# Loading `a` into a block-structured tile, so that one DVE multiply makes AN with its zeros

## The chip, the cores and the metric

The kernel runs on one core of a Trainium2 chip. The metric is the device time of one execution, in microseconds (us). Its engines are PE (matmul), DVE (vector), ACT (scalar), POOL (GpSimd) and SP, which here only issues DMAs; each works through its own instruction order and waits for the others by semaphores.

## The reference

A recurrent attention over 4 batches, 8 heads, 768 steps and a head width of 40, and behind it two feed-forward layers over the 3072 tokens:

```
for t in range(768):
    y[t]  = r[t] @ state
    Sa    = state @ a[t]
    state = state * w[t] - outer(Sa, b[t]) + outer(v[t], k[t])
x = y as (3072, 320)
h = x @ w_in;  x = (max(h,0) + alpha*min(h,0)) @ w_out        # width 2048
out = (silu(x @ w_gate) * (x @ w_val)) @ moe2_w_out           # width 1536
```

All data is float32.

## The kernel before

The 768 steps are cut into 6 blocks of 128 steps; a block and a batch make an item, 24 in all (`order`, m the block, bb the batch). An item's eight heads lie in four pairs: one head of a pair in partitions 0 to 39 (`lo`), the other in 64 to 103 (`hi`), and its 128 steps are two chunks of 64. The step by step recurrence is replaced, within a chunk, by small matrices.

`load` (line 445) brings an item's inputs from HBM: `raw_wa` holds w and a of both halves, `raw_bk` holds b and k. `load_next` is called behind the code that last reads a tile, so the load for a later item waits for that reader. `rset` gives two sets of these tiles for the first eight items and one set afterwards. `prep_a` (492) builds the running products of w: ACT copies w into `wseg` (497), DVE scans it into `rest` (502) and `Wx` (509). Then it makes `AN`, a tile of two halves by 128 partitions: POOL clears the two quarters where half and partitions do not belong together (517), and two DVE multiplies on 64 partitions each write a times Wx into the other two (519). `prep_b` (525) multiplies b and k (`kbt`, 531), forms AN^T-like products on PE (`mnp`, 543), copies masked pieces of them into the cleared quarters of AN (ACT 556, POOL 557), and transposes kbt (571) into `KB` (574). `inverse` (586) inverts a block's triangular matrices in a chain of 31 short DVE steps (604, 612) between transposes (589, 615, 617) and two PE steps (`eps` 625, `dps` 644). `seq` (661) is the recurrence itself over the chunks of an item, as a chain through PE, ACT, DVE and POOL: `sp` 707, `zp` 714, `pp` 724 and 730, `gp` 741, `yp` 756 and 760. Two items run side by side, so there are two such chains.

Beside this, `conv` (187) rewrites the weights into two-part float32r (`narrow`, DVE 172 to 177), and `mlp1` (301) does the first feed-forward layer of a block once its attention is finished: `u` (238) and `d` (243 to 249) matmuls, in 16 groups of eight u and eight d for a block. Where one block's groups end and the next block's begin, the new block's x is fetched from HBM (`fill_x`, 257); below this place is called a seam. The second feed-forward layer (955 to 976) comes last.

The order on each engine is not written out by hand. The code gives every piece a priority (`tc.cur_priority`, `drive`, line 120), and the scheduler that builds the program picks for each engine among what is ready. A small edit can therefore change the order everywhere behind it.

Of the kernel before, what the change touches and what calls it, by code (L numbers as in the profile page):

```python
# [7 lines left out]
F32 = mybir.dt.float32  # L8
# [3 lines left out]
ALU = mybir.AluOpType  # L12
# [22 lines left out]
ANP = 0  # L35
# [27 lines left out]
L = 64  # L63
# [5 lines left out]
def kernel(  # L69
# [15 lines left out]
    nc = tc.nc  # L85
    NM, B, _, D, NP, TB = r.shape
# [3 lines left out]
    CPB = TB // L  # L90
    NSEG = NP * CPB
# [6 lines left out]
    lo, hi = slice(0, 64), slice(64, 128)  # L98
# [275 lines left out]
    def masks():  # L374
        nc.gpsimd.memset(mask, 1.0)
        for p in (lo, hi):
            nc.gpsimd.affine_select(
                out=mask[p], in_=mask[p], compare_op=ALU.is_gt, fill=0.0, base=0,
                pattern=[[1, L]], channel_multiplier=-1,
            )  # L380
        nc.gpsimd.memset(ident, 1.0)
        nc.gpsimd.affine_select(
            out=ident, in_=ident, compare_op=ALU.is_equal, fill=0.0, base=0,
            pattern=[[-1, 128]], channel_multiplier=1,
        )
# [7 lines left out]
    item_x = boot.enter_context(tc.tile_pool(name="item_x", bufs=XI, side="right"))  # L393
    raw = {}
    for j, pool in ((0, rawp), (1, bp)):
        for nm in ("wa", "bk"):
            t = raw[nm, j] = pool.tile([128, 2, NP, TB], F32, name=f"raw_{nm}{j}")
            for n in range(2):
                for q in (1, 3):
                    eng = nc.vector if nm == "wa" and j == 0 else nc.gpsimd  # L400
                    eng.memset(t[32 * q:32 * q + 32, n], 1.0 if (nm, n) == ("wa", 0) else 0.0)
        if j == 0:
            masks()
        tc.cur_priority += 10000
# [3 lines left out]
    for j in range(2):  # L408
        if j < NVT or BVT:
            t = (pers if j < NVT else bp).tile([128, NP, TB], F32, name=f"raw_vt{j}")  # L410
# [16 lines left out]
    for j in range(2):  # L427
        t = pers.tile([128, NG, L], F32, name=f"tt{j}")
        TT.append(t)
    ST = []  # L430
    for j in range(B):
        t = pers.tile([128, NP, 64], F32, name=f"ST{j}")
# [5 lines left out]
    seg = "q p (c t) -> q (p c) t"  # L438
# [3 lines left out]
    def rset(i):  # L442
        return i % 2 if i < EARLY else 0

    def load(i, nm):
        if i >= len(order):
            return
        m, bb = order[i]
        t = raw[nm, rset(i)]
        for h, pr in enumerate(halves):  # L450
            nc.sync.dma_start(out=t[pr], in_={"wa": wa, "bk": bk}[nm][m, bb, h])

    def load_next(i, nm):
        if i < EARLY - 2:
            load(i + 2, nm)
        elif i != EARLY - 1:
            load(i + (2 if i == EARLY - 2 else 1), nm)
# [34 lines left out]
    def prep_a(i):  # L492
        m, bb = order[i]
        it = items[i] = {}
        rw = raw["wa", rset(i)][:, 0]
        w3 = wseg[:, 0:WN].rearrange("p (s t) -> p s t", t=L + 1)
        nc.scalar.copy(out=w3[:, :, 1:L + 1], in_=rw.rearrange(seg, c=CPB)[:, :, ::-1])
        rest = rests[i % 2]
        fl = "p s t -> p (s t)"
        HW = WN // 2  # L500
        for g in range(2):
            nc.vector.tensor_tensor_scan(
                rest.rearrange(fl)[:, g * HW:g * HW + HW], wseg[:, g * HW:g * HW + HW], reset.rearrange(fl),
                0.0, ALU.mult, ALU.add,
            )
        item_p = item_x if i < XI else item_q
        wx = it["Wx"] = item_p.tile([128, NSEG, L + 1], F32, tag="Wx", name="Wx")
        nc.vector.reciprocal(out=first[:, ::-1, 0:1], in_=rest[:, :, L:L + 1])
        nc.vector.tensor_tensor_scan(
            wx.rearrange(fl), wseg[:, WN:0:-1], first.rearrange(fl), 0.0, ALU.mult, ALU.add  # L510
        )
        nc.scalar.copy(out=wx[:, ::-1, L:L + 1], in_=rest[:, :, L:L + 1])
        yield
        ra = raw["wa", rset(i)][:, 1]
        an = it["AN"] = item_p.tile([128, 2, NSEG, L], F32, tag="AN", name="AN")
        for h, pr in ((0, hi), (1, lo)):
            nc.gpsimd.memset(an[pr, h], 0.0)  # L517
        for h, pr in ((0, lo), (1, hi)):
            (nc.gpsimd if i >= B and ANP >> h & 1 else nc.vector).tensor_tensor(
                out=an[pr, h], in0=ra[pr].rearrange(seg, c=CPB), in1=wx[pr, ::-1, 0:L], op=ALU.mult  # L520
            )
        load_next(i, "wa")
        yield

# [256 lines left out]
    def preps(idx):  # L781
        yield from prep_a(idx[0])
        for i in idx:
            ga = prep_a(i + 1) if i + 1 in idx else iter(())
            for _ in prep_b(i):
                next(ga, 0)
                yield

    for i in range(2):
        load(i, "wa")  # L790
        load(i, "bk")
# [79 lines left out]
    for m in range(1, NM):  # L871
# [8 lines left out]
        nm = N_MLP + (1 if FA and m == 1 else 0)  # L880
# [150 lines left out]
```

## Time and profile before

| | |
|---|---|
| three runs, median (lowest to highest) | 1245.16 us (1241.27 to 1247.08) |
| profiled execution, first to last instruction (its span) | 1243.4 us |
| PE busy | 1095.8 us, 88% |
| DVE busy | 781.3 us, 63% |
| ACT busy | 592.6 us, 48% |
| POOL busy | 312.6 us, 25% |
| DMA, mean over the span | 134 GB/s |

The time of the profiled execution beyond its span is not listed; the span lies 1.8 us under the median and between the lowest and the highest run. The page is read by stretches: in the first 80 us there is hardly work for PE, up to about 248 us DVE is nearly full, and from there PE is.

### The profile page before, as it was taken

How to read it: one execution, taken by the hardware profiler on the slowest of the kernel's cores; microseconds unless marked ns; L12 is line 12 of the kernel's file. 1: busy time of each engine (PE TensorE's matmuls, PEld its weight loads, DVE VectorE, ACT ScalarE, POOL GpSimd, SP SyncE). 2: the span in 40 equal slices, each digit the busy share in tenths (PEclk: the TensorE clock that was granted, in tenths of full speed). 3: DMA queues.
4: the chain of work that ended last, by engine and by line, in shares of the span. 5: the costliest groups of instructions: out<-in, count | busy, mean ns of one | idle time of the engine just before them, and what ended most of it. 6: DMA issues, size and time to landing. Idle time of an engine off the chain costs nothing.

```text
span 1243.4 us, 24467 instructions
## 1 busy us (share of the span) xinstructions
PE 1095.8 (88%) x9056; PEld 928.7 (75%) x9056; DVE 781.3 (63%) x1689; ACT 592.6 (48%) x1463; POOL 312.6 (25%) x502
## 2 busy tenths in 40 slices
PE   3345787899799989989999899999999999999998
PEld 2244577777687777777777687888888888888887
DVE  7999999898669758974967444677732323232222
ACT  4547448844763674477455533455432323232222
POOL 9425443613121222252126300334500000000000
PEclk9658697999899999999999999999999999999999
DMA  5534577874545454464448648865210101000000
GB/s 149 168 115 133 180 257 251 263 228 126 161 127 176 134 161 142 144 196 145 145 139 266 201 131 292 283 213 153 73 47 1 47 1 38 1 22 1 22 1 22
DMA packets 92486, 166.36 MB, mean 134 GB/s; under 512 B 12752, under 2 KB 42704, under 8 KB 92368
## 3 DMA queue, kind: packets, MB, share of 16 engines
q1 hardware_dynamic: 84208, 160.87, 41.2%
q10 hardware_dynamic: 8160, 3.93, 1.1%
q8 instruction: 72, 1.18, 0.4%
q14 instruction: 46, 0.38, 0.1%
HBM read 136.98 MB, written 27.79 MB: 133 GB/s over the span
## 4 chain that ended last, share of the span: by engine, by line
PE 52%; DVE 20%; ACT 10%; DMA 8%; issue 6%; POOL 3%; SPq 1%; ACTq 0%; DVEq 0%; POOLq 0%
PE pg L238 10%; PE pv L238 10%; PE u L238 8%; PE o L952 3%; PE o L951 3%; PE o L953 3%; DVE la L612 3%; DVE tmp L604 3%; DMA raw_wa<-in_wa_dram 2%; PE gp L741 2%; PE d L243 2%; DMA xa<-xd 2%; PE d L244 2%; PE d L245 2%; DVE gs L685 2%
## 5 line engine op out<-in xcount | busy, mean ns | idle before, releaser
L184 ACT CAST gh<-g 128x512 fp32r<-128x512 f32 (+1 forms) x176 | 105.9, 602 | 175.2 <-DVE g L967 116.7
L967 DVE TENSOR_TENSOR g<-pv,sg 128x512 f32<-128x512 f32 x72 | 49.8, 691 | 200.1 <-PE pv L238 200.0
L185 DVE TENSOR_TENSOR gl<-g,gh 128x512 fp32r<-128x512 f32 (+1 forms) x176 | 119.5, 679 | 77.0 <-ACT gh L184 76.2
L238 PE MATMUL u<-xh,wt 128*128 128x512 f32 (+1 forms) x416 | 147.6, 397 | 15.9 <-DVE g L278 12.6
L278 DVE SCALAR_TENSOR_TENSOR g<-g,neg,u 128x512 f32<-128x512 f32 (+1 forms) x104 | 72.9, 701 | 63.0 <-ACT g L277 62.4
L238 PEld LDWEIGHTS u<-xh,wt 128*128 128x128 f32 x416 | 79.0, 193 | 34.9 <-DVE g L278 16.8
L238 PE MATMUL pg<-xh,w 128*128 128x512 f32 x288 | 102.0, 394 | 0.7 <-ACT sg L965 0.7
L965 ACT ACTIVATE sg<-pg 128x512 f32<-128x512 f32 x72 | 43.0, 597 | 124.3 <-PE pg L238 124.3
L238 PE MATMUL pv<-xh,w 128*128 128x512 f32 x288 | 100.5, 389 | 0.0
L277 ACT ACTIVATE g<-u 128x512 f32<-128x512 f32 (+1 forms) x104 | 58.7, 564 | 81.6 <-PE u L238 65.0
L543 PE MATMUL mnp<-AN,kbt 128*128 128x128 f32 x384 | 60.7, 311 | 32.1 <-POOL la L591 15.9
L952 PE MATMUL o<-w,gh 128*128 128x320 f32 x288 | 87.7, 309 | 0.0
L951 PE MATMUL o<-w,gh 128*128 128x320 f32 x288 | 87.1, 308 | 0.0
L244 PE MATMUL d<-gl,wt 128*128 128x512 f32 (+1 forms) x208 | 80.9, 391 | 1.2 <-DVE gl L185 1.2
L699 POOL COPY gs<-raw_v 64x160 f32<-64x160 f32 x96 | 42.3, 441 | 157.7 <-PE yp L756 70.1
L543 PEld LDWEIGHTS mnp<-AN,kbt 128*128 128x128 f32 x384 | 54.3, 219 | 36.2 <-POOL AN L517 17.6
L604 DVE TENSOR_TENSOR tmp<-la 128x96 f32<-128x96 f32 (+43 forms) x306 | 78.6, 281 | 3.2 <-POOL la L592 1.3
L238 PE MATMUL u<-xl,wt 128*128 128x512 f32 (+1 forms) x208 | 80.2, 386 | 0.2 <-DVE xl L185 0.2
L612 DVE TENSOR_TENSOR la<-la,tmp 128x96 f32<-128x96 f32 (+43 forms) x306 | 77.6, 278 | 1.9
L245 PE MATMUL d<-gh,wt 128*128 128x512 f32 (+1 forms) x208 | 78.5, 380 | 0.0
L557 POOL TENSOR_SCALAR_AFFINE_SELECT AN<-AN 64x256 f32<-64x256 f32 x96 | 48.5, 505 | 117.9 <-ACT AN L556 88.8
L953 PE MATMUL o<-w,gl 128*128 128x320 f32 x288 | 76.1, 309 | 0.0
(118 smaller groups left out, 2678.6 us busy)
## 6 DMA issues: line engine op xcount, KB each, us to landing
wt<-wd SPq DMA_DIRECT2D x98, 384.0 KB
wt<-wd SPq DMA_DIRECT2D x98, 320.0 KB
wd<-wc SPq DMA_DIRECT2D x24, 384.0 KB
raw<-in_moe_w_out_dram SPq DMA_DIRECT2D x28, 320.0 KB
raw_wa<-in_wa_dram SPq DMA_DIRECT2D x48, 160.0 KB
raw_bk<-in_bk_dram SPq DMA_DIRECT2D x48, 160.0 KB
wd<-wc SPq DMA_DIRECT2D x20, 320.0 KB
raw<-in_moe_w_in_dram SPq DMA_DIRECT2D x16, 256.0 KB
```

The lines of the kernel that those rows point to most:

```text
L184: nc.scalar.copy(out=h, in_=raw)
L185: eng.tensor_tensor(out=l, in0=raw, in1=h.bitcast(F32), op=ALU.subtract)
L238: nc.tensor.matmul(ps, lt, rh, start=(i == 0), stop=(i == len(ops) - 1))
L244: nc.tensor.matmul(ps, wh, gl, start=False, stop=False)
L245: nc.tensor.matmul(ps, wl, gh, start=False, stop=last)
L278: nc.vector.scalar_tensor_tensor(g, g, neg[:, f:f + 1], ps, ALU.mult, ALU.add)
L543: nc.tensor.matmul(ps[:, s].rearrange("p h t -> p (h t)"), kbt[:, g * SH + s].rearrange("p j t -> p (j t)"), an[:, :, g * SH + s, :],)
L604: nc.vector.tensor_tensor(out=tv, in0=ml[:, kk + 1:HALF, kk:kk + 1].to_broadcast([128, nr, ns]), in1=tl[:, kk:kk + 1, c0:c0 + ns].to_broad ...
L612: mark["inv"] = nc.vector.tensor_tensor(out=dst, in0=dst, in1=tv, op=ALU.subtract)
L951: nc.tensor.matmul(ops[q], gh[:, ts], wh, start=first, stop=False)
L952: nc.tensor.matmul(ops[q], gh[:, ts], wl, start=False, stop=False)
L953: nc.tensor.matmul(ops[q], gl[:, ts], wh, start=False, stop=last)
```

## The change

`raw_wa` becomes two tiles. `raw_w` holds w. `raw_a` has two halves over all 128 partitions, is cleared once, and each load writes only a head's own half: zeros stay where half and partitions do not belong together. One DVE multiply over 128 partitions and both halves then writes the whole of AN, its zeros too; the two POOL clears and the two 64-partition multiplies of each item go. Each load of w and a becomes two loads of half the size.

```diff
-        for nm in ("wa", "bk"):
-            t = raw[nm, j] = pool.tile([128, 2, NP, TB], F32, name=f"raw_{nm}{j}")
-            for n in range(2):
+        for nm in ("w", "bk"):
+            sh = [128, 2, NP, TB] if nm == "bk" else [128, 1, NP, TB]
+            t = raw[nm, j] = pool.tile(sh, F32, name=f"raw_{nm}{j}")
+            for n in range(sh[1]):
                 for q in (1, 3):
-                    eng = nc.vector if nm == "wa" and j == 0 else nc.gpsimd
-                    eng.memset(t[32 * q:32 * q + 32, n], 1.0 if (nm, n) == ("wa", 0) else 0.0)
+                    eng = nc.vector if nm == "w" and j == 0 else nc.gpsimd
+                    eng.memset(t[32 * q:32 * q + 32, n], 1.0 if nm == "w" else 0.0)
+        t = raw["a", j] = pool.tile([128, 2, NP, TB], F32, name=f"raw_a{j}")
+        (nc.vector if j == 0 else nc.gpsimd).memset(t, 0.0)
...
-        t = raw[nm, rset(i)]
         for h, pr in enumerate(halves):
-            nc.sync.dma_start(out=t[pr], in_={"wa": wa, "bk": bk}[nm][m, bb, h])
+            if nm == "wa":
+                nc.sync.dma_start(out=raw["w", rset(i)][pr, 0], in_=wa[m, bb, h][:, 0])
+                nc.sync.dma_start(out=raw["a", rset(i)][pr, h], in_=wa[m, bb, h][:, 1])
+            else:
+                nc.sync.dma_start(out=raw["bk", rset(i)][pr], in_=bk[m, bb, h])
...
-        ra = raw["wa", rset(i)][:, 1]
         an = it["AN"] = item_p.tile([128, 2, NSEG, L], F32, tag="AN", name="AN")
-        for h, pr in ((0, hi), (1, lo)):
-            nc.gpsimd.memset(an[pr, h], 0.0)
-        for h, pr in ((0, lo), (1, hi)):
-            (nc.gpsimd if i >= B and ANP >> h & 1 else nc.vector).tensor_tensor(
-                out=an[pr, h], in0=ra[pr].rearrange(seg, c=CPB), in1=wx[pr, ::-1, 0:L], op=ALU.mult
-            )
+        nc.vector.tensor_tensor(
+            out=an, in0=raw["a", rset(i)].rearrange("q h p (c t) -> q h (p c) t", c=CPB),
+            in1=wx[:, ::-1, 0:L].unsqueeze(1).to_broadcast([128, 2, NSEG, L]), op=ALU.mult,
+        )
```

The scheduler's order changes with it on every engine. Lines behind the edit stand three to six numbers higher in the changed kernel (707 becomes 710, for instance). Three places follow; numbers behind a tile's name tell buffers apart.

The first is SP's order at the start of the program, before:

```order
L475 DMA raw_v_164<-in_v_dram 128x320
L475 DMA raw_v_165<-in_v_dram 128x320
L192 DMA raw<-in_moe_w_in_dram 128x2x256
L451 DMA raw_wa_136<-in_wa_dram 40x1024 x2
L451 DMA raw_bk_141<-in_bk_dram 40x1024 x2
L194 DMA raw<-in_moe_w_in_dram 64x256
L451 DMA raw_wa_151<-in_wa_dram 40x1024 x2
```

and of the changed kernel:

```order
L481 DMA raw_v_164<-in_v_dram 128x320
L454 DMA raw_w_136<-in_wa_dram 40x512 x2
L481 DMA raw_v_165<-in_v_dram 128x320
L455 DMA raw_a_144<-in_wa_dram 40x512 x2
L457 DMA raw_bk_139<-in_bk_dram 40x1024
L454 DMA raw_w_136<-in_wa_dram 40x512 x2
L457 DMA raw_bk_139<-in_bk_dram 40x1024
L454 DMA raw_w_151<-in_wa_dram 40x512 x2
```

w of the first item is now asked for ahead of the second `raw_v`; the second load into `raw_w_136`, for item 2, stands ahead of item 1's `raw_w_151`; and the first weights (`raw`) have moved 26 rows back.

The second is DVE's order at the same place, behind its memsets, before:

```order
L502 SCALAR_TENSOR_TENSOR rest_115<-wseg,reset 128x260 x2
L508 RECIPROCAL first<-rest_115 128x8
L531 TENSOR_TENSOR kbt<-raw_bk_141,rest_115 128x2x8x64
L509 SCALAR_TENSOR_TENSOR Wx<-wseg,first 128x520
L172 TENSOR_SCALAR wy<-raw 128x384
L519 TENSOR_TENSOR AN<-raw_wa_136,Wx 64x512 x2
L173 SCALAR_TENSOR_TENSOR wz<-raw,wy 128x384
L502 SCALAR_TENSOR_TENSOR rest_116<-wseg,reset 128x260 x2
```

and of the changed kernel:

```order
L508 SCALAR_TENSOR_TENSOR rest_115<-wseg,reset 128x260 x2
L514 RECIPROCAL first<-rest_115 128x8
L515 SCALAR_TENSOR_TENSOR Wx<-wseg,first 128x520
L521 TENSOR_TENSOR AN<-raw_a_144,Wx 128x1024
L534 TENSOR_TENSOR kbt<-raw_bk_139,rest_115 128x2x8x64
L508 SCALAR_TENSOR_TENSOR rest_116<-wseg,reset 128x260 x2
```

One multiply stands for two, and the weight work (`wy`, `wz`) is gone from between the items: before the first inverse there are now 3 of these instructions instead of 12, and the other nine stand inside the inverse.

The third is PE's order at the seam between blocks 1 and 2 of the first feed-forward layer, before:

```order
L249 MATMUL d_4078<-gl,wt 128x512
L571 MATMUL kbp<-ident,kbt 128x128 x8
L741 MATMUL gp<-rbd_168,pv 128x128 x4
L741 MATMUL gp<-rbd_172,pv 128x128 x4
L543 MATMUL mnp<-AN,kbt 128x128 x8
L756 MATMUL yp<-gs,KB 64x104 x8
L760 MATMUL yp<-rbd_168,s_5668 64x2x64 x4
L756 MATMUL yp<-gs,KB 64x104 x8
L760 MATMUL yp<-rbd_172,s_5679 64x2x64 x4
L571 MATMUL kbp<-ident,kbt 128x128 x8
L238 MATMUL u<-xh,wt 128x512
```

and of the changed kernel:

```order
L249 MATMUL d_4068<-gl,wt 128x512
L733 MATMUL pp<-ident,ut 128x128 x4
L744 MATMUL gp<-rbd_168,pv 128x128 x4
L744 MATMUL gp<-rbd_172,pv 128x128 x4
L759 MATMUL yp<-gs,KB 64x104 x8
L763 MATMUL yp<-rbd_168,s_6023 64x2x64 x4
L238 MATMUL u<-xh,wt 128x512
L759 MATMUL yp<-gs,KB 64x104 x8
L763 MATMUL yp<-rbd_172,s_6031 64x2x64 x4
```

Before, matmuls of the next items' preparation (`mnp`, `kbp`) stand between the steps of the two chains; now the seam comes one item pair later, where no preparation stands. Over the whole order, the last `yp` had 200 u and 208 d matmuls behind it, and now has 224 and 232.

## Rows read from the trace of the kernel before

**Rows 1.** The page: span, and busy time of each engine.

```profile
span 1243.4 us, 24467 instructions
PE 1095.8 (88%) x9056; PEld 928.7 (75%) x9056; DVE 781.3 (63%) x1689; ACT 592.6 (48%) x1463; POOL 312.6 (25%) x502
```

**Rows 2.** Stretches: start:end, length, busy time (instructions) by engine, granted clock, DMA share, GB/s.

```profile
10.25:45.32 35.07, 17.46 (x100) 16.38 (x100) 34.23 (x48) 24.15 (x73) 30.50 (x63) 0.90 0.51 156
45.32:80.09 34.77, 3.46 (x96) 3.31 (x98) 33.67 (x108) 6.59 (x19) 5.29 (x8) 0.53 0.38 130
80.09:248.00 167.91, 128.78 (x1579) 113.31 (x1576) 154.86 (x349) 115.43 (x336) 78.24 (x120) 0.81 0.66 210
...
310.00:330.00 20.00, 12.21 (x207) 10.38 (x203) 11.68 (x19) 13.14 (x37) 3.84 (x8) 0.77 0.66 206
...
440.00:470.00 30.00, 25.75 (x247) 21.15 (x245) 14.40 (x24) 24.44 (x73) 9.53 (x21) 1.00 0.51 158
...
690.00:720.00 30.00, 24.52 (x232) 19.19 (x232) 13.52 (x24) 16.06 (x45) 5.80 (x10) 0.94 0.51 164
720.00:1243.40 523.40, 514.99 (x2674) 443.64 (x2670) 209.00 (x326) 175.33 (x320) 54.33 (x54) 1.00 0.24 79
```

**Rows 3.** Timeline of the start: start, length, instruction, [idle before <- its releaser].

```profile
3.00 0.48 DVE L401 MEMSET raw_wa<- 32x512 f32 x1 [0.16 <-issue]
3.34 0.77 SPq L451 DMA_DIRECT2D raw_wa<-in_wa_dram  x2
...
8.23 1.28 ACT L497 ACT_TABLE_LOAD   x1 [8.23 <-DMA raw_wa<-in_wa_dram]
...
10.25 1.29 DVE L502 TENSOR_TENSOR_SCAN rest<-wseg,reset 128x260 f32<-128x260 f32 x2 [5.99 <-ACT wseg L497]
...
14.38 1.39 DVE L519 TENSOR_TENSOR AN<-raw_wa,Wx 64x512 f32<-64x512 f32 x2
...
15.89 3.49 PEld L543 LDWEIGHTS mnp<-AN,kbt 128*128 128x128 f32 x16 [15.89 <-POOL AN L517]
```

**Rows 4.** DVE's groups up to 250 us: count, busy us, mean ns, idle before.

```profile
L173 DVE SCALAR_TENSOR_TENSOR wz<-raw,wy 128x384 uint32<-128x384 uint32 (+1 forms) x32 | 20.4, 639 | 0.6
...
L519 DVE TENSOR_TENSOR AN<-raw_wa,Wx 64x512 f32<-64x512 f32 x24 | 18.6, 774 | 0.5
...
L531 DVE TENSOR_TENSOR kbt<-raw_bk,rest 128x1024 f32<-128x1024 f32 x12 | 15.3, 1273 | 0.9 <-PE eps L625 0.8
```

**Rows 5.** POOL's clears of AN, the same view up to 250 us.

```profile
L517 POOL MEMSET AN<- 64x512 f32 x28 | 14.8, 528 | 4.2 <-PE zp L714 2.9
```

**Rows 6.** The loads at line 451: SP's issue time, minimum, median and maximum ns.

```profile
L451 SPq DMA_DIRECT2D raw_wa<-in_wa_dram x48: 281/290/457, 3.3 to 547.2; - x48
```

**Rows 7.** What ACT's copy of w (line 497) waited for: us, times.

```profile
  DMA raw_wa<-in_wa_dram: 25.9, 13
```

**Rows 8.** The chain of waits: start, us, what. A 160 KB load and an 80 KB one.

```profile
8.21 4.15 DMA raw_bk<-in_bk_dram
...
316.50 4.24 DMA raw_vt<-in_vt_dram
```

**Rows 9.** Timeline at 315 to 327 us, between two item pairs.

```profile
315.78 0.28 SPq L451 DMA_DIRECT2D raw_wa<-in_wa_dram  x1
...
316.16 0.66 SPq L484 DMA_DIRECT2D raw_vt<-in_vt_dram  x2
...
320.83 0.71 ACT L676 COPY pv<-raw_vt 128x256 f32<-128x256 f32 x2 [4.38 <-DMA raw_vt<-in_vt_dram]
...
326.09 1.11 PE L571 MATMUL kbp<-ident,kbt 128*128 128x128 f32 x4 [7.20 <-ACT AN L556]
```

**Rows 10.** PE's timeline at the last `yp` and in the groups behind it.

```profile
747.17 0.61 PE L760 MATMUL yp<-rbd,s 128*64 128x128 f32 x8
...
749.65 0.39 PE L243 MATMUL d<-gh,wt 128*128 128x512 f32 x1
749.88 0.39 PE L244 MATMUL d<-gl,wt 128*128 128x512 f32 x1
```

More of the change, by code (lines that the diff above doesn't have):

```diff
@@ L494, in prep_a @@
         it = items[i] = {}
-        rw = raw["wa", rset(i)][:, 0]
+        rw = raw["w", rset(i)][:, 0]
         w3 = wseg[:, 0:WN].rearrange("p (s t) -> p s t", t=L + 1)
```

## The prediction

> **What bounds the kernel now.** I read the page first: PE is busy for 1095.8 of 1243.4 us, DVE for 781.3 [rows 1]. Such a share is a mean over stages, so the table of stretches comes next [rows 2]. From 10.25 to 45.32 us, where the first four items are prepared, DVE works 34.23 of 35.07 us, up to 80.09 us (the first inverse) 33.67 of 34.77, and up to 248 us 154.86 of 167.91. DVE sets the pace there, and PE, with little to do, runs mostly at the lower of its two clock levels, 1.2 GHz (granted clock 0.53 in the inverse). From about 250 us PE is the one that is nearly full: after 720 us it works 514.99 of 523.4 us at full clock, so the last 40% of the time is a sum of matmuls that this edit does not touch. Between these, two places where PE stands idle are to be seen: 310 to 330 us (12.21 of 20 busy) and 690 to 720 us (24.52 of 30). The end moves by what DVE saves before about 250 us, by what PE's idle time gains or loses between 250 and 750 us, and by nothing else that I can see.
>
> **DVE's multiplies.** Before 250 us there are 24 of them for 12 items, of 774 ns on average; kbt, which is the same kind of multiply on 128x1024 with a broadcast operand, took 1273 ns [rows 4]. One for two saves 2 x 774 - 1273 = 275 ns an item, 12 x 0.275 = 3.3 us. DVE is over 90% busy there [rows 2], so I count all of it; the bounds are 0, if the saved time falls into waits, and 3.3. The other 12 items lie in the stretch where PE sets the pace; what DVE saves there I count at nothing. It is covered by PE's own work; if DVE is the later one in places, another 12 x 0.275 = 3.3 us can come out at most.
>
> **The start.** SP issues the first `raw_wa` at 3.34 us, behind the last of four DVE clears of that tile, which ends at 3.48 us; ACT, and then DVE's first scan at 10.25 us, wait for its landing [rows 3]. In the changed order w needs two clears only, of 0.48 us each, and stands ahead of the second `raw_v`, so it can go at about 2.2 us: 1.2 us sooner, and the whole chain of DVE behind it with it. The clear of `raw_a` falls into the 6 us in which DVE waits. Against this, item 1's w is now queued behind a load that waits for ACT's copy of item 0, and the weights come later, so that DVE may find nothing to fill its gaps with. Moving the nine weight instructions behind the first transposition changes no sum (their price is at most 9 x 0.639 = 5.8 us [rows 4], done later). I take -1.2, with bounds of -3 and +2 (a landing of some 4 us [rows 8] that is half hidden).
>
> **POOL's clears.** 28 of 528 ns, 14.8 us, go before 250 us [rows 5]. The first PE work at 15.89 us is put down to such a clear, but the second DVE multiply ended at 14.38 + 1.39 = 15.77 us [rows 3]: were the clear gone, AN would have been ready no sooner. POOL has slack in every other stretch, and I count 0; the bounds are -2 and 0. The clears also were the first writers of an AN buffer and waited on POOL for its last reader `zp`. That wait goes over to DVE, whose multiplies already had to follow the same reader; the eight buffers make it an old event. Count 0.
>
> **The loads.** 48 loads of 160 KB become 96 of 80 KB. SP gives each some 290 ns [rows 6], 13.9 us more in all, of a queue that mostly waits for others. An 80 KB load landed after 4.24 us, a 160 KB one after 4.15 us [rows 8]: half the size lands no sooner, and the gain of asking for w sooner, once ACT has copied it and not only behind AN, pays for the extra issues. Count 0, bounds -3 and +7.5 (a rival below). The Trainium skill (DMA: Bandwidth & Descriptors, section Bandwidth) speaks against this part: it wants transfers batched to a megabyte and calls those under 64 KB dominated by descriptors; by its table an 80 KB transfer moves well under half as many bytes per us as a large one. By that rule the sum would be the third rival's below instead of mine. The trace agrees that an 80 KB load is no quicker than one of twice the size.
>
> **What the new order does to PE.** Two things. At 320.83 us ACT waits 4.38 us for `raw_vt`, which stood on SP behind a `raw_wa` that waited for DVE; PE's next matmul waits 7.20 us with it [rows 9]. In the changed order eight more u and a dozen d matmuls stand at this place, which do not need that copy; but ACT must still evict for them. I take half of the stall, -3.6 us, bounds -7.2 and 0. On the other side, the seam between blocks 1 and 2 loses its cover. Where it has preparation around it, 440 to 470 us, PE idles 30 - 25.75 = 4.25 us; the bare seam at 690 to 720 us idles 30 - 24.52 = 5.48 us [rows 2]. The preparation keeps its own waits wherever it stands, so an additional bare seam costs between 5.48 - 4.25 = 1.2 and 5.5 us. I take +4, nearer the upper end for that reason.
>
> **The sum:** -3.3 - 1.2 - 3.6 + 4.0 = -4.1 us. The span of the profiled execution is 1243.4 us [rows 1], the median of the runs 1245.16, 1.8 us more; what lies around the span does not change. So 1239.3 us of span, **1241.1 us** as a median. A change below 0.5%, 6.2 us, is about what a measurement of this kernel cannot tell from none. The forecast is no change that can be told, on the faster side.
>
> **Rivals.**
>
> *The early lead is kept and the stall goes as a whole.* If the added u and d matmuls cover 320 us fully and the seam that has lost its cover costs nothing new, the sum is -3.3 - 1.2 - 7.2 = -11.7: **1233.5 us**. For it speaks that DVE is so full early on, and that PE idles at 310 to 330 us for one copy. Against it: PE must wait at some seam for x from HBM.
>
> *PE's work is left over behind the attention.* The changed order has 24 u and 24 d matmuls more behind the last `yp`. They follow each other at 749.88 - 749.65 = 0.23 us [rows 10], so 48 x 0.23 = 11.0 us. If PE was the limit up to there, the attention ends that much sooner and nothing is lost. If its two chains set their own pace, with ACT, DVE and POOL in each step, the attention gains only the early lead and half of the stall, less the seam, 4.1 us, and the end comes 11.0 - 4.1 = 6.9 us later: **1252.1 us**. It decides from the point where the last `yp` (747.17 us before) starts less than 11.0 - 6.2 = 4.8 us sooner. For it speaks that PE idles in many small waits between 250 and 750 us; against it, that most of those stretches are over 90% busy.
>
> *The halved loads are late.* ACT's copy of w waits 13 times, 25.9 us in all, for its load [rows 7]. Two more issues ahead of each, 2 x 0.29 us, make 13 x 0.58 = 7.5 us; were it all on the path, the start and DVE's savings of 4.5 us would be given back: 1245.2 - 4.5 + 7.5 = **1248.2 us**. Against it, w no longer has to wait for AN. A rule of the Trainium skill lies close to this, the one on batching in DMA: Bandwidth & Descriptors.
>
> That the edit does not do what it says is ruled out: the order shows the one multiply and no clears.
>
> **How the numbers follow.** The forecast has 0.45: 0.36 within 0.5%, 0.08 faster than that and 0.01 slower, since its terms lean to faster. The first rival has 0.28 (0.27 faster, 0.01 within), the second 0.22 (0.20 slower, 0.02 within), the third 0.05, within. Together: faster 0.35, within 0.5% 0.44, slower 0.21. The range must take in the first rival with DVE's later 3.3 us (1233.5 - 3.3 = 1230.2) and the second, with the start's worse bound (+2 where -1.2 was taken: 1252.1 + 3.2 = 1255.3): 1230 to 1255. The forecast's own part of it is some 1236 to 1248.
>
> **What would show it.** DVE's first scan before 9.3 us, 24 multiplies of AN of about 1.25 us, and the first transposition of the inverse at least 3 us sooner than the weight work that was moved behind it explains, would bear out the first two terms. PE's idle time between 310 and 330 us (7.8 us before) and at three seams tells the next two. The start of the last `yp` tells forecast and second rival apart: at 735 us or sooner the left-over work was paid for. The prediction is wrong if PE's idle time between 250 and 750 us changes by over 8 us, or if a new wait for `raw_w` or `raw_a` stands among the longest on ACT or DVE.

## The result, and the profile of the changed kernel

The changed kernel takes 1254.69 us (median of four runs, 1253.07 to 1254.95); the kernel before, run beside it, 1244.79 (1241.27 to 1247.08). The ratio is 1.0084, with a 95% interval of 1.0066 to 1.0102: slower by about 10 us. The forecast was 1241.1 us and no change. The time lies inside the range and 2.6 us from the second rival's, but the runs will show that this is not by that rival's sum.

The page of the changed kernel, its span and busy times:

```profile
span 1252.8 us, 24424 instructions
...
PE 1105.7 (88%) x9056; PEld 934.5 (75%) x9056; DVE 776.3 (62%) x1664; ACT 593.2 (47%) x1463; POOL 301.5 (24%) x453
```

Against [rows 1], DVE works 5.0 us less and POOL 11.1 us less, as the edit should have it. The span is 9.4 us longer. PE has the same 9056 matmuls, and its idle time (span less busy) is 147.1 us where it was 147.6. What has grown is PE's *busy* time, by 9.9 us. The same matmuls took longer, and the view of the core's granted clock (its mean share of full speed) shows the likely reason, before:

```profile
core 0: 1243.4 us, clock 0.949
```

and of the changed kernel:

```profile
core 0: 1252.8 us, clock 0.937
```

The clock has two levels, 2.4 and 1.2 GHz. Laid over the records of the matmuls, the clock's records (they begin 16 to 24 us into a trace) show PE working 80 us at the lower level before and 98 us now. Half of the 18 us more is 9, nearly the whole difference of this pair of executions. 8 of the 18 lie before 250 us, 7 between there and the last `yp`, 3 behind it. The experiments will show that this pair makes the clock's part look larger than it usually is.

The same stretches as in [rows 2], changed kernel (start:end, length, busy time by engine, granted clock, DMA share, GB/s):

```profile
10.25:45.32 35.07, 17.28 (x132) 15.99 (x132) 28.65 (x43) 25.36 (x78) 25.08 (x41) 0.83 0.50 155
45.32:80.09 34.77, 0.83 (x32) 0.84 (x34) 33.70 (x106) 5.25 (x13) 6.94 (x9) 0.50 0.33 114
80.09:248.00 167.91, 128.19 (x1557) 112.24 (x1552) 152.53 (x336) 112.62 (x325) 82.15 (x110) 0.76 0.66 212
310.00:330.00 20.00, 18.82 (x150) 15.94 (x150) 11.45 (x14) 14.68 (x43) 1.64 (x4) 0.83 0.56 174
440.00:470.00 30.00, 28.28 (x280) 24.33 (x278) 17.64 (x49) 20.78 (x60) 7.46 (x18) 1.00 0.44 139
690.00:720.00 30.00, 26.24 (x241) 20.19 (x241) 12.02 (x24) 13.54 (x37) 3.25 (x9) 0.93 0.51 154
720.00:1252.80 532.80, 520.88 (x2636) 446.17 (x2632) 210.26 (x321) 176.24 (x320) 52.45 (x48) 0.99 0.24 79
```

The stall between 310 and 330 us is gone (18.82 us busy, before 12.21). At 440 to 470 us PE works 28.28 us (before 25.75), but the seam that stood there before has moved behind 470 us. The matmuls that wait for the new block's x, before:

```profile
460.75 0.50 PE L238 MATMUL u<-xl,wt 128*128 128x512 f32 x1 [0.23 <-DVE xl L185]
```

and of the changed kernel:

```profile
470.69 0.50 PE L238 MATMUL u<-xh,wt 128*128 128x512 f32 x1 [0.47 <-ACT xh L184]
...
477.57 1.22 PE L238 MATMUL u<-xst,wt 128*128 128x512 f32 x2 [1.01 <-DVE xst L268]
```

A stretch that holds the seam of either kernel, before and changed:

```profile
440.00:480.00 40.00, 35.75 (x322) 29.38 (x321) 22.86 (x58) 30.78 (x90) 11.85 (x25) 1.00 0.48 147
```

```profile
440.00:480.00 40.00, 36.09 (x356) 29.35 (x356) 27.02 (x71) 25.94 (x73) 10.06 (x26) 0.96 0.45 139
```

PE idles 3.91 us in it, before 4.25. Early on it is the other way: DVE works 28.65 of the first 35.07 us where it worked 34.23, and from 80 to 248 us the clock is 0.76 where it was 0.81.

The timeline of the start, DVE's instructions and one issue of SP (start, length, instruction, idle time before and its releaser):

```profile
7.68 1.29 DVE L508 TENSOR_TENSOR_SCAN rest<-wseg,reset 128x260 f32<-128x260 f32 x2 [3.70 <-POOL raw_bk L402]
...
10.55 1.23 DVE L521 TENSOR_TENSOR AN<-raw_a,Wx 128x1024 f32<-128x1024 f32 x1
...
30.25 0.40 SPq L192 DMA_DIRECT2D raw<-in_moe_w_in_dram  x1
...
34.47 1.29 DVE L508 TENSOR_TENSOR_SCAN rest<-wseg,reset 128x260 f32<-128x260 f32 x2 [2.63 <-ACT wseg L503]
...
41.49 1.93 DVE L592 STREAM_TRANSPOSE la<-tt 128x1024 f32<-128x1024 f32 x1 [1.95 <-ACT tt L555]
```

The first scan starts 2.57 us sooner than in [rows 3]. But the weights are first asked for at 30.25 us, so that DVE finds nothing to put into its waits of 2.63 and 1.95 us. The last row is the inverse's first transposition. Before, it stood here:

```profile
45.32 1.94 DVE L589 STREAM_TRANSPOSE la<-tt 128x1024 f32<-128x1024 f32 x1
```

DVE's group for the one multiply up to 250 us, and what ACT's copy of w waited for over the whole span (us, times, longest):

```profile
L521 DVE TENSOR_TENSOR AN<-raw_a,Wx 128x1024 f32<-128x1024 f32 x12 | 16.1, 1345 | 0.1
```

```profile
ACT L503 <- DMA raw_w<-in_wa_dram: 5.7, 1, 5.7
...
ACT wseg L503 <- DMA raw_w<-in_wa_dram: 4.6, 4, 1.5
```

PE's timeline at and behind the last `yp`:

```profile
739.07 0.61 PE L763 MATMUL yp<-rbd,s 128*64 128x128 f32 x8
...
749.88 0.55 PE L238 MATMUL u<-xh,wt 128*128 128x512 f32 x1 [2.17 <-DVE g L278]
750.23 0.63 PE L238 MATMUL u<-xl,wt 128*128 128x512 f32 x1
750.65 1.05 PE L238 MATMUL u<-xh,wt 128*128 128x512 f32 x2
...
770.34 0.47 PE L238 MATMUL u<-xh,wt 128*128 128x512 f32 x1 [2.05 <-DMA wt<-wd]
770.64 0.59 PE L238 MATMUL u<-xl,wt 128*128 128x512 f32 x1
771.03 1.06 PE L238 MATMUL u<-xh,wt 128*128 128x512 f32 x2
```

The last `yp` comes 8.1 us sooner than in [rows 10]. Behind it PE stops twice for over 2 us, and after each stop matmuls follow each other at 0.42 us (750.23 to 750.65) or 0.39, not at 0.23 [rows 10]. The kernel before has one such stop, 2.22 us at 757.51 us. From the last `yp` to the second layer's first matmul pass 115.1 us, before 97.0: 18.1 us more for 48 matmuls more. Cut at these two places, the 9.4 us are -8.1, +18.1 and, in the second layer, -0.7.

### The profile page after: what moved, and what is told of

Same layout as the page of the kernel before. It is cut to its first block, busy times and chain, and to the rows that moved or that the text cites. A ratio compares the mean times of both kernels' runs of the same rounds, so it can differ in the third digit from the quotient of the medians.

```text
span 1252.8 us, 24424 instructions
## 1 busy us (share of the span) xinstructions
PE 1105.7 (88%) x9056; PEld 934.5 (75%) x9056; DVE 776.3 (62%) x1664; ACT 593.2 (47%) x1463; POOL 301.5 (24%) x453
## 4 chain that ended last, share of the span: by engine, by line
PE 47%; DVE 10%; ACT 7%; DMA 6%; issue 2%; SPq 1%; POOL 1%; ACTq 0%; DVEq 0%; POOLq 0%
PE pg L238 10%; PE pv L238 10%; PE u L238 5%; PE o L955 3%; PE o L954 3%; PE o L956 3%; PE d L243 1%; DMA wt<-wd 1%; PE d L244 1%; DVE g L278 1%; PE d L245 1%; DVE tmp L607 1%; DVE la L615 1%; PE gp L744 1%; PE mnp L546 1%
## 5 line engine op out<-in xcount | busy, mean ns | idle before, releaser
L238 PE MATMUL u<-xh,wt 128*128 128x512 f32 (+1 forms) x416 | 150.9, 404 | 13.4 <-DVE g L278 8.8
L560 POOL TENSOR_SCALAR_AFFINE_SELECT AN<-AN 64x256 f32<-64x256 f32 x96 | 56.4, 587 | 110.6 <-ACT AN L559 85.0
L546 PE MATMUL mnp<-AN,kbt 128*128 128x128 f32 x384 | 60.7, 312 | 21.6 <-DVE kbt L534 18.1
L185 POOL TENSOR_TENSOR wc<-wz,wc 128x384 fp32r<-128x384 f32 (+3 forms) x60 | 60.2, 1014 | 66.9 <-ACT wc L184 53.1
```

Source lines behind the costliest of these rows:

```text
L185: eng.tensor_tensor(out=l, in0=raw, in1=h.bitcast(F32), op=ALU.subtract)
L238: nc.tensor.matmul(ps, lt, rh, start=(i == 0), stop=(i == len(ops) - 1))
L546: nc.tensor.matmul(ps[:, s].rearrange("p h t -> p (h t)"), kbt[:, g * SH + s].rearrange("p j t -> p (j t)"), an[:, :, g * SH + s, :],)
```

## The experiments

Theories: **A**, the halved loads with their extra issues cost the time. **C**, the wide multiply, or the missing clears, cost it. **B**, the work costs what the prediction worked out, and the loss comes from the order that the scheduler found for the changed program. Later B is split, and D and E join, in the expectations. The kernel before ran beside each group (medians 1244.8 to 1248.3 us), so ratios to it are compared.

**One load per half again.** One tile of three columns: a strided load writes w and the head's own half of a; the one multiply stays.

```diff
-                nc.sync.dma_start(out=raw["w", rset(i)][pr, 0], in_=wa[m, bb, h][:, 0])
-                nc.sync.dma_start(out=raw["a", rset(i)][pr, h], in_=wa[m, bb, h][:, 1])
+                nc.sync.dma_start(out=raw["wa", rset(i)][pr, 0:h + 2:h + 1], in_=wa[m, bb, h])
```

> w and a stay in one tile of three columns (w, a of the first head, a of the second), so each half needs one load of 160 KB as before; the one DVE multiply and the missing clears stay as in the changed kernel. Theory A (the halved loads and their extra issues on SP cost the time): 1240 to 1245 us, the gain of DVE's multiplies kept. Theory B (the work costs what was worked out, and the loss is in the scheduler's new order, to be seen in the feed-forward matmuls left behind the last yp: here 504, 96 more than before, where the changed kernel has 456): 1251 to 1265 us. Theory C (the one multiply or the missing clears themselves cost): about 1254 us, as the changed kernel.

Measured: 1277.33 us, ratio 1.0228 (1.0189 to 1.0267). The loads are whole again and the kernel is slower still: A's 1240 to 1245 us did not come, and the time lies above B's 1251 to 1265 too. The order is another one here as well, so this run alone does not price the extra issues.

**The halved loads alone**, with the old clears and the two multiplies.

```diff
+        for h, pr in ((0, hi), (1, lo)):
+            nc.gpsimd.memset(an[pr, h], 0.0)
+        for h, pr in ((0, lo), (1, hi)):
+            (nc.gpsimd if i >= B and ANP >> h & 1 else nc.vector).tensor_tensor(
```

> The loads are split into w and a as in the changed kernel, but the two multiplies on 64 partitions and POOL's clears of AN are those of before. Theory A: 1254 us or more. Theory B (488 matmuls left behind the last yp, 80 more than before): 1250 to 1262 us. Theory C: within 4 us of before.

Measured: 1256.03 us, ratio 1.0071 (1.0044 to 1.0099). The loss is there without the wide multiply and with the clears: C is not needed for it. By itself this would fit A; the run before it and the two behind it don't.

**Two kernels whose order alone differs** from the kernel before. The first gives the first weights the preparation's priority, the second writes the load of b and k ahead of that of w and a.

```diff
-    drive((preps(range(B)), B * N_PREP, HP), (take(c1, EC0), EC0 + .1, 0))
+    drive((preps(range(B)), B * N_PREP, HP), (take(c1, EC0), EC0 + .1, HP))
```

```diff
     for i in range(2):
+        load(i, "bk")
         load(i, "wa")
-        load(i, "bk")
```

> The kernel before with no change in its work: only the first two weight conversions get the priority of the preparation, so that the scheduler puts out another order (456 matmuls left behind the last yp, 48 more than before, as many as the changed kernel has). Theories A and C: within 4 us of before, since loads, multiplies and clears are those of before. Theory B: 5 to 12 us slower.

> The kernel before with no change in its work: the first loads of b and k are written ahead of those of w and a, and the scheduler puts out another order (504 matmuls left behind the last yp, 96 more than before). Theories A and C: within 4 us of before. Theory B: 6 to 20 us slower.

Measured: 1272.85 us, 1.0190 (1.0150 to 1.0229), and 1275.15 us, 1.0213 (1.0173 to 1.0253). With no change in work at all, the order costs over twice what the edit did. Both are above the 5 to 12 and 6 to 20 us that were expected from the number of matmuls left behind. The page of the second:

```profile
span 1271.2 us, 24462 instructions
...
PE 1101.1 (87%) x9056; PEld 928.7 (73%) x9056; DVE 782.7 (62%) x1689; ACT 593.7 (47%) x1463; POOL 310.4 (24%) x502
```

PE is idle for 170.1 us, 22.5 more than before. Part of that is behind the last `yp`, where 504 u and d matmuls are left and wait for their weights (`wt`):

```profile
769.80 0.47 PE L243 MATMUL d<-gh,wt 128*128 128x512 f32 x1 [1.38 <-DMA wt<-wd]
...
773.57 0.47 PE L238 MATMUL u<-xh,wt 128*128 128x512 f32 x1 [1.72 <-DMA wt<-wd]
```

**DVE's saving with the order held.** Once the scheduler has set the order of the kernel before, the scans of every later item are made shorter; no instruction moves.

```diff
+def shorter(o):
+    ap = [list(a) for a in o.ap]
+    ap[-1][1] = 156
+    return o.__replace__(ap=ap)
...
+                    if seen > 4:
+                        blk.instructions[i] = x.__replace__(
+                            outs=tuple(shorter(o) for o in x.outs),
+                            ins=tuple(shorter(o) if hasattr(o, "ap") else o for o in x.ins))
```

> The kernel before, with the order on every engine held word for word; from the third item on, each of the two scans into rest (line 502) covers 156 columns in place of 260. This leaves out part of the running products of w, from item 2 on. At 0.73 to 0.84 us for a scan of 260 columns a pair gets some 0.6 us shorter: about twice the 0.275 us that the one multiply saves an item, in ten items before 250 us, 6 us of DVE. Theory B (the edit's savings are real, the loss comes from the new order): with the order held the end comes 3 to 6 us sooner, 1238 to 1242 us where the kernel before has 1244.8, and the second half of the items adds nothing. Rival D (what DVE saves before 250 us falls into waits, also with the order held): 1243 to 1246 us.

Measured: 1243.9 us beside 1248.25, ratio 0.9965 (0.9944 to 0.9986).

```profile
span 1241.2 us, 24467 instructions
...
PE 1095.7 (88%) x9056; PEld 928.4 (75%) x9056; DVE 771.1 (62%) x1689; ACT 591.6 (48%) x1463; POOL 312.9 (25%) x502
```

DVE works 10.2 us less than in [rows 1]; up to 250 us its scans into `rest` take 13.6 us in place of 18.5. The end comes 0.35%, 4.4 us, sooner than in the kernel before beside it; the two profiled spans differ by 2.2 us. PE's busy time is the same to 0.1 us. The 1243.9 us themselves lie in D's range, since the kernel before ran 3.5 us longer in this group than it was expected to; the difference to it is what B forecast (3 to 6 us) and D did not. In the order of the kernel before, DVE's early time reaches the end.

**Other orders of the changed kernel.** One or two constants of the priorities are altered, the work stays.

```diff
-XPRI = 1000
+XPRI = 3000
```

> The changed kernel with one constant altered, the lift of x's transfers in priority (1000 to 3000); the work is the same, the order is not: 184 u and 192 d matmuls stand behind the last yp, where the changed kernel has 224 and 232 and the kernel before 200 and 208. Up to the end of block 1 it does 229 u and d matmuls (changed kernel 200, before 240). Theory B1 (what is left behind the last yp decides, at about 0.31 us each): last yp within 740 to 752 us, 88 to 94 us from it to the second layer, no wait of u or d for wt behind the last yp, 1230 to 1243 us in all. Theory B2 (the matmuls that were not done in PE's idle time before 250 us decide): between the two kernels and nearer the one before, 1245 to 1250 us. Theory A or C (the halved loads or the wide multiply cost it): 1252 us or more, since both are still in.

```diff
-PRI = 3000
+PRI = 4000
```

> The changed kernel with the priority of the preparation at 4000 in place of 3000; same work. 200 u and 208 d matmuls stand behind the last yp, exactly as in the kernel before, but up to the end of block 1 only 208 u and d are done (changed kernel 200, before 240). Theory B1 (what is left behind the last yp decides): 97 us from the last yp to the second layer, 1236 to 1245 us. Theory B2 (the early matmuls decide): the loss stays, the last yp comes later instead, 1250 to 1256 us. Theory A or C: 1252 us or more.

```diff
-SQ = 3000
+SQ = 2500
-HP2 = 3000
+HP2 = 2000
```

> The changed kernel with the attention's priority at 2500 in place of 3000 and that of the second preparation at 2000 in place of 3000; same work. 176 u and 176 d matmuls stand behind the last yp, and up to the end of block 1 275 u and d are done (before 240): fewer left and more done early than in either kernel. Theories B1 and B2 both say faster than the changed kernel: the attention has the lower rank, so the last yp at 748 to 760 us, 80 to 86 us from it to the second layer, 1230 to 1244 us. If the lower rank lets the two chains wait for PE, the last yp comes after 765 us and nothing is gained, 1250 us. Theory A or C: 1252 us or more.

Measured: 1.0001 (0.9979 to 1.0024), 1.0100 (1.0066 to 1.0134) and 1.0155 (1.0119 to 1.0190). The first has the edit whole and gives the loss back: A and C fall. B1 falls: with as few left behind the last `yp` as before (408) the second loses 1.0%, its last `yp` coming at 765.8 us (before 747.5), and with the fewest of all (352) the third is the slowest, its last `yp` at 771.6 us. B2 fits the first, has the second right in sign (1261 us, expected at most 1256) and misses the third, which had done most early. Neither count tells the time.

**Is there a fixed cost of the edit?** The same constants go into the kernel before, so that pairs differ by the edit alone; two more orders of the changed kernel are tried for a fast one. (Theory **E**: a fixed cost of the edit.)

> The kernel before with the same one constant as e6_lift_3000 (the lift of x's transfers, 1000 to 3000); no change in work. 240 u and 248 d matmuls stand behind the last yp, 220 are done up to the end of block 1. It is the partner of e6_lift_3000 (1248.8 us, ratio 1.000). Theory B (the edit itself is worth a few us at most, and the order that the scheduler happens to find is worth up to 25): no fixed difference between partners; with 80 matmuls more left behind than before, 1255 to 1276 us, so that here the kernel with the edit is the faster one. Theory E (the edit costs what it cost in the first pair, 10 us, whatever the order): 1236 to 1242 us.

> The kernel before with the constant of e7_prep_4000 (priority of the preparation 4000 in place of 3000); no change in work. 192 u and 200 d matmuls stand behind the last yp, 216 are done up to the end of block 1. Partner of e7_prep_4000 (1261.1 us). Theory B: its own order decides; e7 had the same few left and its last yp came 18 us later than before, so 1248 to 1268 us here, and no fixed sign against its partner. Theory E (the edit costs 10 us): 1248 to 1254 us.

> The changed kernel with the lift of x's transfers at 3000 and the priority of the second preparation at 2000 (both were other values, 1000 and 3000); same work. 192 u and 200 d matmuls behind the last yp, 259 done up to the end of block 1, 697 at the end of block 3 (before: 408 left, 240 and 691). Theory B: an order whose progress is that of the kernel before, with the edit's saving of 4 us on top: 1238 to 1248 us, low clock between 80 and 250 us no longer than before (granted clock 0.80 or more), PE's idle time 145 to 150 us. Theory E: 1252 us or more.

> The changed kernel with the priority of the second preparation at 2000 in place of 3000; same work. 224 u and 232 d matmuls behind the last yp as in the changed kernel, but 253 done up to the end of block 1 (changed kernel 200, before 240) and 691 at the end of block 3 (641, 691). If what was not done early makes the loss: 1240 to 1249 us. If what stands behind the last yp makes it: 1252 to 1258 us, as the changed kernel. If neither count tells the time, anything from 1245 to 1275 us, and then PE's idle time and its time at the lower clock must account for the difference.

> The kernel before with the two constants of e8_two_lower (attention's priority 2500, second preparation's 2000); no change in work. Partner of e8_two_lower (ratio 1.0155). 200 u and 208 d matmuls behind the last yp, as before. Theory B (no fixed difference between partners, the order decides): 1245 to 1272 us. Theory E (the edit costs 0.8% whatever the order): 1.0075, 1256 to 1259 us.

> The kernel before with the constant of e12_hp_2000 (second preparation's priority 2000); no change in work. Partner of e12_hp_2000 (ratio 1.0053). Its order is close to that of the kernel before: the same 408 matmuls behind the last yp, 240 done up to the end of block 1, 691 at the end of block 3. Theory B: 1243 to 1255 us, since PE's idle time and its time at the lower clock should be near those of the kernel before. Theory E (the edit costs 0.8%): 0.997, 1241 to 1245 us.

> The kernel before with the two constants of e11_both_hp (lift of x's transfers 3000, second preparation's priority 2000); no change in work. Partner of e11_both_hp (ratio 0.9971). 208 u and 216 d matmuls behind the last yp, 254 done up to the end of block 1. Theory B: 1245 to 1270 us, no better than its partner. Theory E (the edit costs 0.8%): 0.989, 1232 to 1236 us, the fastest of all.

Measured, as ratios to the kernel before, in pairs:

| constants | without the edit | with the edit | with less without |
|---|---|---|---|
| as they were | 1 | 1.0084 (1.0066 to 1.0102) | +0.8% |
| XPRI 3000 (e9, e6) | 1.0161 (1.0120 to 1.0203) | 1.0001 (0.9979 to 1.0024) | -1.6% |
| PRI 4000 (e10, e7) | 1.0145 (1.0125 to 1.0165) | 1.0100 (1.0066 to 1.0134) | -0.4% |
| SQ 2500, HP2 2000 (e13, e8) | 1.0051 (1.0035 to 1.0066) | 1.0155 (1.0119 to 1.0190) | +1.0% |
| HP2 2000 (e14, e12) | 1.0016 (0.9997 to 1.0034) | 1.0053 (1.0036 to 1.0069) | +0.4% |
| XPRI 3000, HP2 2000 (e15, e11) | 1.0042 (1.0027 to 1.0057) | 0.9971 (0.9953 to 0.9989) | -0.7% |

Three pairs go up, three down; the mean is -0.1%, with a scatter of 1.0% from pair to pair. E falls: it wanted +0.8% each time. A saving of 0.3% could not be seen in six such pairs either. e12 was a miss for the early matmuls: it had as much done early as the kernel before and still took 1253.5 us. Its time is the one that the count behind the last `yp` wanted, but that count had failed in e7 and e8, and e10, with 392 left, is slower by 1.4%. e11 came out within its range, but not by the way expected: PE idles 136.3 us there (expected 145 to 150), and the granted clock from 80 to 250 us is 0.79 (expected 0.80 or more).

**DVE's saving in the order of the changed kernel**, the same cut of the scans.

> The changed kernel with its order held word for word and the scans into rest shortened from item 2 on, exactly as e5_half_scans did to the kernel before: this leaves out part of the running products of w. In e5 DVE's busy time fell by 10.2 us and the end came 0.35% sooner. Theory B (the saving reaches the end in any order that has DVE full early on): ratio to the kernel before 1.003 to 1.006, that is 3 to 6 us under the changed kernel's 1254.7. Rival D (in this order DVE waits for data early on, 21 us up to the end of block 0 where it waited 15 before, so that the saving falls into waits): 1.007 to 1.010, no change against the changed kernel.

Measured: ratio 1.0049 (1.0031 to 1.0067), in B's range and 0.35% under the changed kernel's 1.0084. But the two ratios are to two groups of runs of the kernel before, whose medians differ by 0.28%. As times, the two kernels are 1253.5 and 1254.7 us, their spans average 1252.6 us each, and in the profiled pair DVE works 7.9 us less while PE idles 5.6 us more. That the saving reaches the end in this order too is not shown, and D is not out.

**What the runs have in common.** For each profiled execution: PE's idle time (span less PE busy, both from the page), and the time that PE worked at 1.2 GHz by the clock's records. The last two columns are, against the kernel before, the change of idle time plus half that of the low time, and the change of the span.

| kernel | idle, us | at 1.2 GHz, us | idle + half | span |
|---|---|---|---|---|
| before | 147.6 | 80 | | 1243.4 |
| changed | 147.1 | 98 | +8.7 | +9.4 |
| e1 | 163.3 | 90 | +21.0 | +28.1 |
| e2 | 147.4 | 100 | +10.1 | +13.8 |
| e3 | 155.8 | 112 | +24.1 | +25.7 |
| e4 | 170.1 | 83 | +24.1 | +27.8 |
| e5 | 145.5 | 79 | -2.3 | -2.2 |
| e6 | 149.6 | 85 | +4.5 | +3.7 |
| e7 | 157.9 | 81 | +10.8 | +16.6 |
| e8 | 156.8 | 83 | +10.6 | +20.4 |
| e9 | 159.4 | 113 | +28.2 | +25.8 |
| e10 | 149.1 | 115 | +18.9 | +19.7 |
| e11 | 136.3 | 110 | +3.9 | +0.6 |
| e12 | 155.8 | 91 | +13.9 | +9.9 |
| e13 | 142.3 | 102 | +5.6 | +6.4 |
| e14 | 140.0 | 97 | +0.8 | -0.4 |
| e15 | 145.1 | 114 | +14.3 | +12.2 |
| e16 | 152.7 | 89 | +9.4 | +10.7 |

In 14 of 17 the two columns agree within 4 us; e1, e7 and e8 are 7.1, 5.8 and 9.8 us longer than the sum. In e8 PE's busy time grew by 11.2 us with only 3 us more at the lower clock, so it grows by something else as well, which no run separates. e10 is the plainest case: no u or d matmul more is left behind than before, PE's idle time is 1.5 us longer, and the span 19.7 us:

```profile
span 1263.1 us, 24496 instructions
...
PE 1114.0 (88%) x9056; PEld 941.5 (75%) x9056; DVE 785.7 (62%) x1689; ACT 595.4 (47%) x1463; POOL 314.1 (25%) x502
```

Its busy time has grown by 18.2 us with the same matmuls. The fastest order with the edit, e11, shows that the two trade against each other:

```profile
span 1244.0 us, 24434 instructions
...
PE 1107.7 (89%) x9056; PEld 940.5 (76%) x9056; DVE 776.1 (62%) x1664; ACT 592.6 (48%) x1463; POOL 288.5 (23%) x453
```

Against the kernel before it has 11.3 us less idle time and 30 us more at the lower clock. It is the changed kernel with XPRI 3000 and HP2 2000, 0.3% faster than the kernel before (interval 0.1 to 0.5%) and 1.1% faster than the changed kernel (0.9971 / 1.0084). It was picked out of six orders with the edit, which flatters it.

The table is an account, not a test: no edit changed the clock alone, and the two columns must agree wherever PE's busy time grows because of the clock only. Nearer to a test are the runs of the kernel before, 76 in all beside the experiments, always in its one order. Their mean clock lies between 0.936 and 0.950 and their span between 1240.4 and 1251.9 us: the 21 at 0.946 or above average 1243.7 us, the 25 at 0.941 or below 1248.6. So with work and order the same, a low clock goes with a longer time. But it is not the whole of the loss. The changed kernel's four runs (clock 0.937 to 0.943) average 1252.6 us, and the kernel before at 0.937 to 0.943 averages 1247.6: at a like clock some 5 us stay. The profiled pair sets a run of the kernel before with a high clock (0.949) against the changed kernel's lowest (0.937). Against all 76 runs (median 1248 us), beside which the changed kernel did not run, its loss would be 0.5%.

That the order makes the loss is shown (e3, e4, e6 and the pairs). That it does so in part by way of the lower clock is read from the records; how much of a usual run's loss that is, and what the rest is, stays open.

## Why the prediction was wrong, by its steps

- **DVE's multiplies, -3.3 us: right in kind, a little too large.** Up to 250 us the group fell from 18.6 us [rows 4] to 16.1, 2.5 us. That DVE's saving there reaches the end is shown by e5 for the order of the kernel before: 0.35% for a cut of 4.9 us in that stretch. For the changed order e16 leaves it open.
- **The start, -1.2 us: wrong.** The scan came 2.57 us sooner, which is more than forecast, but the rest was given back. The risk that was named and left at a bound ("DVE may find nothing to fill its gaps with") is what happened: the first transposition comes 3.83 us sooner (41.49 us, before 45.32), no more than the moved weight work (at most 5.8 us) explains, and the first inverse ends at 81.0 us, before 80.1. By the end of block 0's attention DVE had waited 21.3 us (before 15.4 at that point) and that end came at 192.6 us, before 182.0.
- **POOL's clears, 0:** not tested by itself; in e2, which keeps them, the loss is nearly the same.
- **The loads, 0: held.** ACT's copy of w waits 10.3 us, 5 times, where it waited 25.9, 13 times [rows 7]; in e2, with halved loads too, it waits 5.6 us, once, and in e1, with whole ones, 36.1 us, 13 times. So the third rival is out: the halved loads are waited for less, since w is asked for sooner. The rule of the Trainium skill (DMA: Bandwidth & Descriptors, section Bandwidth) by which smaller transfers lose doesn't decide here.
- **The stall, -3.6 us:** PE gained nearly the whole of it, 6.6 us busy more in those 20 us. **The bare seam, +4.0 us:** too large. The two waits for x at 470.69 and 477.57 us are 1.48 us, where the one before was 0.23: +1.25 us, the lower bound. Over 440 to 480 us PE idles no more than before.
- **The step that failed** is in the first paragraph: the end moves "by what PE's idle time gains or loses between 250 and 750 us, and by nothing else that I can see". Between 250 and 750 us idle time fell, 35.4 us from 40.9, and over the whole span it is what it was; yet the end came 9.4 us later in the profiled pair. The sign that was set for being wrong, a change of over 8 us there, did not show. What the sum had no term for is PE's busy time, which grew by 9.9 us. The granted clock stood in [rows 2] and was read as a sign that PE had little to do, not as a price (and "mostly at the lower" holds for the inverse's 0.53, not for 0.90 and 0.81): 18 us more at 1.2 GHz are 9 us of the 9.9.
- **The second rival** (1252.1 us) gave nearly the measured time by a step that did not happen as written. By its own rule it was out: the last `yp` came 8.1 us sooner, beyond the 4.8 us from which the work left over counts as paid for (if short of the 735 us that was named as the sign of it), so its sum would have been 11.0 - 8.1 = +2.9 us. The 48 matmuls cost 18.1 us in place of 11.0: PE's idle time there is 6.2 us, before 2.2, and it worked 6.8 us there at the lower clock, before 3.4. So it had the place where the time shows, but both of its sizes were wrong, and that they nearly made up for each other is luck. And as a rule it fails in e7, e8 and e10.
- **The chances.** The forecast and two of its rivals treated the new order as the old one with a few terms moved. Seven other orders without the edit lie from 1.0016 to 1.0213, most of them with a change of one constant. All seven lie above 1 (e14's interval alone takes it in): the order of the kernel before is a good one, and a new one is likelier to lose than to win. An edit worth 0.3% that makes the scheduler draw a new order is a draw from such a spread, and nothing in the cases stood for that: slower at 0.21 was too low.

## What to carry to other kernels

Where a scheduler sets the order, an edit has two effects: the work that it saves, and a new order. The first is measured by changing the length of instructions after the order is set (0.35% here, in the order of the kernel before); the second by trying the edit and the kernel before under several settings, in pairs. And where PE is the limit late and waits early, cost its busy time too: the change of idle time plus half that of the time that it works at the lower clock gave the change of the span to within 4 us in 14 of 17 kernels here. One profiled execution is one draw of the clock, though: the kernel before alone ran from 0.936 to 0.950.

## What was not expected of the hardware

PE's idle time and its count of matmuls can stay the same while its busy time grows by 9.9 us (18.2 in e10). A stop of 2 us can cost more than itself: behind the one at 749.88 us the matmuls went at 0.42 us in place of 0.23 up to about 753 us; behind e4's stops of 1.38 and 1.72 us they went at 0.22 and 0.23. The Trainium skill (TensorE: Matmul & The Clock Gate, section Terms) puts the penalty at the throttled time times one less the clock's share, here a half. Over the whole span the mean clocks of 0.949 and 0.937 make 127 and 158 us at the lower level; by that rule the 31 us more would cost 15.5 us. The two spans differ by 9.4: only the part in which PE had work seems to count, 18 us of the 31. And in one and the same order the clock differs from run to run: the spans of the kernel before lie up to 11 us apart with it.
